# Linear attention and two MLPs: the root by Ln and Exp, other distances in the second batch, hosted x over another tile, earlier stores of the first weights

## The chip, the cores and the metric

The kernel runs on one core of a Trainium2 chip. What is measured is the device time of one execution in microseconds (us). A core has TensorE (PE: matmuls, with their weight loads as PEld), VectorE (DVE), ScalarE (ACT), GpSimd (POOL), and SyncE (SP), whose queue issues most of the DMAs; ACT's queue issues the others. TensorE writes to PSUM, which has eight banks here, and DVE and ACT read its results from there. Each engine works through its instructions in the order in which they stand in its queue: an instruction that waits holds up those behind it.

## The reference

Eight batches of eight heads, 576 rows, 64 columns per head; then two MLPs over 4608 tokens, 512 wide with 2048 inside.

```
kv  = einsum('bhsd,bhse->bhde', k, v)
out = einsum('bhsd,bhde->bhse', q, kv)
x   = out / sqrt(mean(out * out, axis=-1) + 1e-06) * g_norm    # heads side by side: 4608 x 512
h   = x @ w_in1;  g = h if h >= 1, 0 if h <= -1, else (h + 1)**2 / 4;  x = g @ w_out1
h   = x @ w_in2;  g = max(h, 0)**2;                            out = g @ w_out2
```

The weights come in as 64-bit floats, read as pairs of 32-bit words.

## The kernel before, in words

**Products.** A tile that must be multiplied with good precision is split into a high part of type fp32r and a low part, the difference. `mm3` adds three matmuls (high by high, high by low, low by high). Some small products of the attention are done instead as one matmul in full fp32, which the profile shows as two instructions.

**The stages.** The first five batches (`PLAIN`) go through the first MLP plainly, one block each: in each of 16 steps `h_stage` makes one 128-wide slice of h (12 matmuls), `g_stage` splits g, and `out_stage` adds its product into four accumulators (12 matmuls). The first six steps of the first block run ahead of its out stages. After these five blocks come six pairs of batches (`PAIRS`) and a rest, in which both MLPs are done with seven products for a two by two block product (`in_phase`, `out_phase`). These take weights and sums of weights from a DRAM copy in split form (`wsd`), by `load_w2` into tiles `ws`.

**Slots.** A slot is half a step: slot 2t follows the h stage of step t, slot 2t+1 its out stage, and a block has 32 slots. `hook` puts work into a slot. This gives the program's order; a planner then arranges the instructions of each engine by its own estimate of when each is ready, so the order in a queue can differ from that of the program.

**Attention.** A batch has four pairs of heads. Batch 0 goes ahead of the first block (`attention_first` with `t_first`, `o_first`, `r_first`). Batches 1 to 4 go along in the block before their own, and batches 5 to 7 are hosted in the first two pairs: twelve pairs of heads, whose x goes to DRAM (`xpd`, `xrd`). For one pair of heads, starting at slot s: `kv_stage` (k by v into one bank, copied to SBUF), `t_stage` (q transposed by DVE), two `o_stage` halves (q by kv; ACT writes the squares and the product with g, which stands in `gvec` times -0.5), and `r_stage`. For all batches but 0 the PSUM banks are the two buffers of the tag `at`.

**r_stage.** For each half, a matmul with a tile of 1/64 gives the mean square m in a bank (`pr`); ACT makes y = 1/sqrt(|m + 1e-6|) from it, over the squares' tile. Then t = y squared (ACT), o = o * y (DVE), and one Newton step: `newton` makes t = (m + 1e-6) * t (it reads the banks, and frees them), `norm` makes (t - 3) * o, which with gvec's -0.5 is x. It goes over t, and for hosted batches over o, from which it is stored.

**Distances.** In `attention`, pair j starts at s = base + int(every * j), with every 6.7 for batches 1 to 4 and 6 for hosted ones. The o halves are at s+4 and s+5, r at s+8 (s+7 for hosted). Batch 1 calls `kv_stage` for each pair at its s; the others for two pairs at once. Loads stand seven slots ahead of their use (q of hosted pairs: five). `WHOLE` names pairs (1,0) and (1,1), whose squares too are multiplied in full fp32.

**First weights.** `split_w` (slots 2i and 2i+1 of the first block, a few steps ahead of use) makes the split tiles of the first MLP's weights: 16 of w_in, 16 of w_out. Their copies in DRAM are stored by SyncE's queue (line 159). The last nine of w_out (`TAIL`) are stored right after they are split and read again as `wt` tiles by `load_tail` in each later block (line 294). The other 23 are stored by `keep_first`, number j at slot 14 + 2j. Stores of all columns are 512 KB, those of half 256 KB. From the second block on, the second MLP's weights are prepared beside the blocks (`prep_load`, `prep_narrow`, `prep_sums`, `prep_split`; loads at lines 316 and 321) and stored by ACT's queue.

Of the kernel before, what the change touches and what calls it, by code (L numbers as in the profile page):

```python
# [10 lines left out]
F32 = mybir.dt.float32  # L11
F32R = mybir.dt.float32r
AF = mybir.ActivationFunctionType
ALU = mybir.AluOpType
I32 = mybir.dt.int32
BF16 = mybir.dt.bfloat16

# [53 lines left out]
def linear_attention_rms_two_mlps(  # L71
# [112 lines left out]
    ident = ap2.tile([P, P], F32, tag="q", name="ident")  # L184
    ones = const.tile([P, P], F32R, name="ones")
    gvec = const.tile([P, 1], F32, name="gvec")
    epsb = const.tile([P, 1], F32, name="epsb")
    halfb = const.tile([P, 1], F32, name="halfb")
    kv0 = wp.tile([P, NP, P], F32, tag=f"w1_{NF - 1}", name="kv0")
    rests = [const.tile([P, 2, 2, D], F32, name=f"rest{i}") for i in range(2)]  # L190
    kvbd = [const.tile([P, P], F32, name=f"kvbd{i}") for i in range(2)]

    engines = {"A": nc.scalar, "D": nc.vector, "P": nc.gpsimd}
    turns = {op: [itertools.cycle(e) for e in by.split()] for op, by in ENGINES.items()}
# [5 lines left out]
    def engine(op, phase):  # L200
        return engines[next(turns[op][min(phase, 2)])]
# [9 lines left out]
    def copy(e, dst, src):  # L211
        if e is nc.scalar:
            return e.copy(dst, src)  # L213
        if e is nc.vector:
            return e.tensor_copy(dst, src)
        return scaled(e, dst, src, 1.0)
# [249 lines left out]
    def kv_stage(*pairs):  # L466
        ps = bank(pairs[0][0], "pkv_{}_{}".format(*pairs[0]))
        for n, (b, hp) in enumerate(pairs):
            kt, vt = kvm.pop((b, hp))
            r = kvr.pop((b, hp))  # L470


            for c in range(MR + 1):
                for j in range(2):
                    s = slice(j * D, (j + 1) * D)
                    d = slice(n * P + j * D, n * P + (j + 1) * D)
                    lhs, rhs = (kt[:, c, j], vt[:, j, c, :]) if c < MR else (r[0][:, j], r[1][:, j])
                    nc.tensor.matmul(ps[s, d], lhs, rhs, start=c == 0, stop=c == MR)  # L478
        for n, (b, hp) in enumerate(pairs):
            for j in range(2):  # L480
                s = slice(j * D, (j + 1) * D)
                d = slice(n * P + j * D, n * P + (j + 1) * D)
                if b == 0:
                    copy(engine("kv_hi", b), kv0[s, hp, s], ps[s, d])
                    continue
                if (b, hp) in WHOLE:
                    copy(engine("kv_hi", b), kvw[s, hp % 2, s], ps[s, d])
                    continue
                copy(engine("kv_hi", b), kvbd[turn[b, hp] % len(kvbd)][s, s], ps[s, d])

    def t_first(hp):
        qT = scratch(hp, "qT")
# [22 lines left out]
    def newton(t, m):  # L515
        nc.vector.scalar_tensor_tensor(t, m, 1e-6, t, op0=ALU.add, op1=ALU.mult)

    def norm(dst, t, o):
        nc.vector.scalar_tensor_tensor(dst, t, -3.0, o, op0=ALU.add, op1=ALU.mult)

    marks = []

    def r_first(hp):
        y, o = og.pop((0, hp))
        t = scratch(hp, "t")
        ms = []
        for half in range(2):
            ps = bank(0, f"pr_0_{hp}_{half}")
            m = ps[:, :U]
            nc.tensor.matmul(m, ones.bitcast(F32), y[:, half], start=True, stop=True)  # L530
            nc.scalar.activation(y[:, half], m, AF.Abs_reciprocal_sqrt, bias=epsb)
            ms.append(m)
        square(engine("y", 0), t, y)
        nc.vector.tensor_tensor(o, o, y, ALU.mult)
        for half in range(2):
            newton(t[:, half], ms[half])
        norm(t, t, o)
        n = TB // 2
        rem = xrem[0][:, hp, :].rearrange("p (h r) -> p h r", h=2)
        nc.gpsimd.tensor_copy(rem, t[:, :, n:])  # L540
        x = xs[1, 0][hp].rearrange("p a (h n) -> p a h n", h=2)
        marks.append(split(x, t[:, :, :n], "x", 0))


    def t_stage(b, hp):
        work = [ap1.tile([P, S], F32, tag=f"wk{n}", name=f"wk{n}_{b}_{hp}") for n in range(2)]
        qT = ap1.tile([P, S], F32, tag="hl0", name=f"qT_{b}_{hp}")
        nc.vector.transpose(qT, qs.pop((b, hp)))
        hl[b, hp] = (work, qT)

    def o_stage(b, hp, half):
        work, qT = hl[b, hp]
        whole = (b, hp) in WHOLE
        kv = kvw[:, hp % 2, :] if whole else kvbd[turn[b, hp] % len(kvbd)]
        c = slice(half * U, (half + 1) * U)
        ps = bank(b, f"po_{b}_{hp}_{half}")
        nc.tensor.matmul(ps[:, :U], kv, qT[:, c], start=True, stop=True)  # L557
        if whole:
            nc.scalar.activation(work[0][:, c], ps[:, :U], AF.Square)
            scaled(engine("o", b), work[1][:, c], ps[:, :U], gvec)  # L560
            return
        if half == 0:

            og[b, hp] = [ap1.tile([P, S], F32R, tag="wk2", name=f"s2_{b}_{hp}")]
        s2 = og[b, hp]
        nc.scalar.activation(s2[0][:, c], ps[:, :U], AF.Square)
        nc.scalar.activation(work[0][:, c], ps[:, :U], AF.Square)
        scaled(engine("o", b), work[1][:, c], ps[:, :U], gvec)
        if half == 1:
            s2.append(ap1.tile([P, S], F32R, tag="hl1", name=f"s2lo_{b}_{hp}"))  # L570
            lo = engine("sq_lo", b)
            lo.tensor_tensor(s2[1], work[0], s2[0].bitcast(F32), ALU.subtract)

    def r_stage(b, hp):
        (y, o), _ = hl.pop((b, hp))
        if (b, hp) in WHOLE:
            products = [(ones.bitcast(F32), y)]
        else:
            products = [(ones, s2) for s2 in og.pop((b, hp))]
        ms = []  # L580
        for half in range(2):
            c = slice(half * U, (half + 1) * U)
            ps = bank(b, f"pr_{b}_{hp}_{half}")
            m = ps[:, :U]
            for n, (one, s2) in enumerate(products):
                nc.tensor.matmul(m, one, s2[:, c], start=n == 0, stop=n == len(products) - 1)  # L586
            nc.scalar.activation(y[:, c], m, AF.Abs_reciprocal_sqrt, bias=epsb)
            ms.append((c, m))
        pool, tag = (ap1, "wk2") if b < PLAIN else (ap2, "q")
        t = pool.tile([P, S], F32, tag=tag, name=f"t_{b}_{hp}")  # L590
        square(engine("y", b), t, y)
        nc.vector.tensor_tensor(o, o, y, ALU.mult)
        for c, m in ms:
            newton(t[:, c], m)
        if b < PLAIN:
            norm(t, t, o)
            nc.gpsimd.tensor_copy(xrem[b][:, hp, :], t[:, TB:])
            split(xs[1, b][hp], t[:, :TB], "x", b)
            return
        norm(o, t, o)  # L600
        nc.sync.dma_start(xpd[b][:, hp, :], o[:, :TB])
        nc.sync.dma_start(xrd[:, hp, b, :], o[:, TB:])

    def new_x(L, b):
        xs[L, b] = [
# [23 lines left out]
    def attention(base, every, order):  # L629

        slots = []
        for j, (b, hp) in enumerate(order):
            s = base + int(every * j)
            turn.setdefault((b, hp), len(turn))
            if b == 1:
                slots += [(max(0, s - 7), load_kv, b, hp), (s, kv_stage, (b, hp))]
            elif j % 2 == 0:
                two = order[j : j + 2]
                turn.setdefault(two[-1], len(turn))
                slots += [(max(0, s - 7), load_kv, *i) for i in two]  # L640
                slots.append((s - (1 if j else 0) - (b < PLAIN and j > 0), kv_stage, *two))
            slots += [
                (max(0, s - (7 if b < PLAIN or j < 2 else 5)), load_q, b, hp),
                (s, t_stage, b, hp),
                (s + 4, o_stage, b, hp, 0),
                (s + 5, o_stage, b, hp, 1),
            ]
            late = 8 if b < PLAIN else 7
            if j == 0 and b < PLAIN:
                slots.append((s + late, begin, b))  # L650
            slots.append((s + late, r_stage, b, hp))
        if b < PLAIN:
            slots.append((2 * NF * b + 2, store_xrem, b))
        return slots

    def store_xrem(b):
# [426 lines left out]

    jobs = [(8, store_xrem, 0)]
    for b in range(1, PLAIN):
        jobs += attention(2 * NF * (b - 1), 6.7, [(b, hp) for hp in range(NP)])
    for job in sorted(jobs, key=lambda j: j[0]):
        hook(*job)
    for i in range(NF):
# [10 lines left out]
    last = 2 * (PLAIN - 1) * NF  # L1100
    kept = [(w, f) for f in range(NF) for w in range(2) if w == 0 or f < NF - TAIL]
    for j, (w, f) in enumerate(kept):
        hook(14 + 2 * j, keep_first, w, f)

    units = (
# [41 lines left out]
            else:  # L1147
                hook(last + 25, *job)

    nc.scalar.preload_act_table_set("abs_reciprocal_sqrt_and_small")  # L1150
    load_first()
    for f, w in ((2, 0), (3, 0), (0, 1), (4, 0), (1, 1), (5, 0), (2, 1), (6, 0), (3, 1)):
        load_w(1, f, w)
# [12 lines left out]
    for j in range(2):  # L1166
        s = slice(j * D, (j + 1) * D)
        nc.vector.memset(ones[s, s].bitcast(F32), 1.0 / D)
    for t in kvbd:
        nc.vector.memset(t, 0.0)  # L1170
    for t in rests:
        nc.gpsimd.memset(t, 0.0)
    nc.gpsimd.memset(kv0, 0.0)
    nc.vector.tensor_scalar_mul(gvec, gvec, -0.5)
    nc.vector.memset(epsb, 1e-6)
    nc.vector.memset(halfb, 0.5)

    kvw = ap1.tile([P, 2, P], F32, tag="hl1", name="kvw")
# [128 lines left out]
```

## Time and profile before

| | before |
|---|---|
| median of 3 runs | 1578.41 us (1578.3 to 1580.91) |
| the profiled execution's own time | 1577.31 us |
| its span | 1575.5 us |
| PE busy | 1544.7 us, 98% |
| DVE busy | 1169.7 us, 74% |
| ACT busy | 896.1 us, 57% |
| HBM over the span | 245 GB/s |

Busy time is the time in which at least one instruction of the engine runs; matmuls are pipelined, so TensorE can be busy and still not at its peak. Times in the trace are counted from the start of the span. In the rows, "L516" is line 516 of the kernel, "po<-qT,kvbd" reads "tile po written from tiles qT and kvbd", and a bracket with an arrow says how long the engine was idle before the instruction and what ended that.

### The profile page before, as it was taken

The page shows a single profiled execution, that of the slowest core. Times are in us where ns is not written, and L with a number is a line of the kernel's source. Part 1 is how long each engine was busy: PE and PEld are TensorE (multiplying, and loading weights), DVE is VectorE, ACT ScalarE, POOL GpSimd, SP SyncE. Part 2 cuts the span into 40 slices and gives each one's busy share as a digit, 9 for nine tenths or more (in the row PEclk, how much of TensorE's full clock was granted, in tenths as well). Part 3 has the DMA queues.
Part 4 walks back from the last instruction along what each step waited for, and adds up shares of the span by engine and source line. Part 5 has one row for each costly group of instructions (what it writes and reads, how often), then busy time and mean ns, then how long its engine had stood idle before and what let it go on. Part 6 is the DMA issues. An engine that isn't in the chain of part 4 may idle for free.

```text
span 1575.5 us, 22117 instructions
## 1 busy us (share of the span) xinstructions
PE 1544.7 (98%) x7581; PEld 1268.8 (81%) x7581; DVE 1169.7 (74%) x2033; ACT 896.1 (57%) x1693; POOL 10.8 (1%) x30
## 2 busy tenths in 40 slices
PE   9999989999999999998999999999999999999999
PEld 5777768887877788787778888888888888888899
DVE  6975777776789668964789788868884597559666
ACT  5875756666656556734566466546653464446354
POOL 0000000000000000000000000000000000000000
PEclk9999999999999999999999999999999999999999
DMA  9776899897799967789867877776776676977797
GB/s 282 199 231 208 239 338 293 278 288 235 237 341 343 334 200 212 243 226 220 250 187 234 229 240 244 223 218 196 245 233 207 198 242 198 243 243 214 223 391 249
DMA packets 330911, 388.14 MB, mean 246 GB/s; under 512 B 197808, under 2 KB 223408, under 8 KB 330800
## 3 DMA queue, kind: packets, MB, share of 16 engines
q1 hardware_dynamic: 299904, 330.63, 70.1%
q10 hardware_dynamic: 30896, 56.11, 9.8%
q8 instruction: 60, 0.98, 0.2%
q14 instruction: 51, 0.42, 0.1%
HBM read 300.42 MB, written 86.25 MB: 245 GB/s over the span
## 4 chain that ended last, share of the span: by engine, by line
PE 87%; DMA 4%; DVE 4%; ACT 3%; issue 1%; SPq 1%; ACTq 0%; DVEq 0%
PE ph L858 31%; PE po L858 31%; PE acc L234 11%; PE ph L234 10%; PE po L557 2%; DMA wt<-wsd 1%; PE pkv L478 1%; PE pr L586 1%; DMA wsd<-s 1%; DVE s L182 1%; DMA ws<-wsd 1%; DMA v<-in_v_dram 0%; DVE u L684 0%; DMA k<-in_k_dram 0%; DVE x L787 0%
## 5 line engine op out<-in xcount | busy, mean ns | idle before, releaser
L858 PE MATMUL ph<-x,ws 128*128 128x512 f32 (+1 forms) x2352 | 508.7, 377 | 0.5 <-DVE u L684 0.5
L858 PEld LDWEIGHTS ph<-x,ws 128*128 128x128 f32 x2352 | 421.0, 190 | 81.0 <-DVE u L684 0.9
L858 PE MATMUL po<-t,ws 128*128 128x512 f32 x2016 | 462.4, 390 | 0.8 <-DVE t L787 0.8
L858 PEld LDWEIGHTS po<-t,ws 128*128 128x128 f32 x2016 | 377.9, 188 | 80.7 <-DVE t L787 2.2
L787 DVE TENSOR_TENSOR t<-g,t 128x512 fp32r<-128x512 f32 (+1 forms) x336 | 216.3, 649 | 86.4 <-ACT t L213 82.9
L213 ACT CAST t<-g 128x512 fp32r<-128x512 f32 (+1 forms) x336 | 195.5, 590 | 117.7 <-PE po L858 63.3
L234 PE MATMUL ph<-x,w 128*128 128x512 f32 x960 | 241.2, 397 | 8.5 <-DVE u L684 7.4
L234 PEld LDWEIGHTS ph<-x,w 128*128 128x128 f32 x960 | 178.4, 188 | 52.3 <-DVE u L684 10.7
L935 ACT ACTIVATE g<-h 128x512 f32<-128x512 f32 (+1 forms) x120 | 70.6, 589 | 111.8 <-DVE h L924 111.8
L234 PE MATMUL acc<-gs,w 128*128 128x512 f32 x528 | 132.4, 395 | 0.4 <-ACT w L213 0.2
L924 DVE CUSTOM_DVE_ANT_0 h<-ph,e 128x512 f32<-128x512 f32 (+1 forms) x120 | 76.3, 637 | 61.0 <-PE ph L858 56.9
L914 DVE TENSOR_TENSOR e<-ph,e 128x512 f32<-128x512 f32 (+1 forms) x112 | 72.3, 650 | 61.3 <-PE ph L858 56.5
L234 PEld LDWEIGHTS acc<-gs,w 128*128 128x128 f32 x528 | 98.2, 188 | 22.2 <-ACT w L213 0.9
L234 PE MATMUL acc<-gs,wt 128*128 128x512 f32 x432 | 107.6, 398 | 3.9 <-DVE gs L226 2.2
L234 PEld LDWEIGHTS acc<-gs,wt 128*128 128x128 f32 x432 | 82.0, 191 | 22.3 <-DVE gs L226 2.6
L213 ACT CAST gs<-u 128x512 fp32r<-128x512 f32 x80 | 49.7, 622 | 65.0 <-DVE u L684 48.8
L682 ACT ACTIVATE u<-ph,halfb 128x512 f32<-128x512 f32 x80 | 55.2, 690 | 48.0 <-PE ph L234 36.1
L213 ACT CAST x<-xr 128x512 fp32r<-128x512 f32 (+1 forms) x98 | 57.2, 589 | 43.1 <-DVE xr L838 24.3
L226 DVE TENSOR_TENSOR gs<-u,gs 128x512 fp32r<-128x512 f32 x80 | 54.9, 687 | 27.0 <-ACT gs L213 26.5
L684 DVE SCALAR_TENSOR_TENSOR u<-u,ph 128x512 f32<-128x512 f32 x80 | 54.3, 681 | 24.1 <-ACT u L220 24.0
L787 DVE TENSOR_TENSOR x<-xr,x 128x512 fp32r<-128x512 f32 (+1 forms) x98 | 63.1, 648 | 2.6 <-ACT x L213 2.6
L911 ACT COPY e<-ph 128x512 f32<-128x512 f32 (+1 forms) x56 | 30.8, 554 | 56.4 <-PE ph L858 49.5
(127 smaller groups left out, 1547.0 us busy)
## 6 DMA issues: line engine op xcount, KB each, us to landing
ws<-wsd SPq DMA_DIRECT2D x392, 512.0 KB, 4.4
wsd<-s ACTq DMA_DIRECT2D x96, 512.0 KB, 5.5
wt<-wsd SPq DMA_DIRECT2D x36, 512.0 KB, 5.5
raw<-in_moe_w_in_dram SPq DMA_DIRECT2D x32, 512.0 KB, 6.6
raw<-in_moe_w_out_dram SPq DMA_DIRECT2D x32, 512.0 KB, 6.5
xr<-x1d SPq DMA_DIRECT2D x36, 256.0 KB, 5.4
out_dram<-ov SPq DMA_DIRECT2D x142, 64.0 KB, 3.5
wsd<-w SPq DMA_DIRECT2D x17, 512.0 KB, 4.2
```

The lines of the kernel that those rows point to most:

```text
L213: return e.copy(dst, src)
L226: lo = engine(op + "_lo", phase).tensor_tensor(t[:, 1, :], src, t[:, 0, :].bitcast(F32), ALU.subtract)
L234: nc.tensor.matmul(dst, wt(a), xt(c), start=first and n == 0, stop=last and n == 2)
L557: nc.tensor.matmul(ps[:, :U], kv, qT[:, c], start=True, stop=True)
L682: nc.scalar.activation(u, ps, AF.Relu, bias=halfb, scale=0.5)
L684: nc.vector.scalar_tensor_tensor(u, u, 1.0, ps, op0=ALU.min, op1=ALU.max)
L787: engine2(op + "_lo").tensor_tensor(t[:, 1, :], src, t[:, 0, :].bitcast(F32), ALU.subtract)
L858: nc.tensor.matmul(ps, wt(a), xt(c), start=first and n == 0 and i == 0, stop=last and n == len(lhs) - 1 and i == 2, skip_group_check=True,)
L911: nc.scalar.copy(e[i, 1], bank)
L914: nc.vector.tensor_tensor(e[i, p], bank, e[i, 1], ALU.add)
L924: nc.vector._custom_dve(TENSOR_ADD_SAT, out=h, in0=bank, in1=add, s0=float("inf"), s1=0.0)
L935: nc.scalar.activation(g, h, AF.Square)
```

## The change

The root: y is made as exp(-0.5 * ln(m + 1e-6)), Ln for each half from the bank, Exp once over both halves. Ln's input is scaled by 2^-44, and Exp's bias takes that back. The product of o and y is gone; `norm` makes t = (t - 3) * y and then t = o * t, and hosted x is stored from t. ACT's table is preloaded for the new functions.

The second batch (batch 1): for pairs (1,2) and (1,3) kv and the transposed q are split, and o is made by `mm3`. For all its pairs every is 7, the o halves are at s+3 and s+4, r at s+6. The other batches keep their distances.

The stores: `keep_first` number j stands at slot 16 + int(2j / 3).

```diff
-    epsb = const.tile([P, 1], F32, name="epsb")
+    lnb = const.tile([P, 1], F32, name="lnb")
+    expb = const.tile([P, 1], F32, name="expb")
...
+    kv1 = const.tile([P, 2, P], F32R, name="kv1")
...
-                copy(engine("kv_hi", b), kvbd[turn[b, hp] % len(kvbd)][s, s], ps[s, d])
+                if b > 1:
+                    copy(engine("kv_hi", b), kvbd[turn[b, hp] % len(kvbd)][s, s], ps[s, d])
+                    continue
+                t = kv1
+                copy(engine("kv_hi", b), t[s, 0, s], ps[s, d])
+                nc.vector.tensor_tensor(t[s, 1, s], ps[s, d], t[s, 0, s].bitcast(F32), ALU.subtract)
...
-    def norm(dst, t, o):
-        nc.vector.scalar_tensor_tensor(dst, t, -3.0, o, op0=ALU.add, op1=ALU.mult)
+    def norm(t, y, o):
+        nc.vector.scalar_tensor_tensor(t, t, -3.0, y, op0=ALU.add, op1=ALU.mult)
+        nc.vector.tensor_tensor(t, o, t, ALU.mult)
... r_first
-            nc.scalar.activation(y[:, half], m, AF.Abs_reciprocal_sqrt, bias=epsb)
+            nc.scalar.activation(y[:, half], m, AF.Ln, bias=lnb, scale=LN_SCALE)
             ms.append(m)
+        nc.scalar.activation(y, y, AF.Exp, bias=expb, scale=-0.5)
         square(engine("y", 0), t, y)
-        nc.vector.tensor_tensor(o, o, y, ALU.mult)
         for half in range(2):
             newton(t[:, half], ms[half])
-        norm(t, t, o)
+        norm(t, y, o)
... t_stage
-        qT = ap1.tile([P, S], F32, tag="hl0", name=f"qT_{b}_{hp}")
+        if b > 1 or (b, hp) in WHOLE:
+            qT = ap1.tile([P, S], F32, tag="hl0", name=f"qT_{b}_{hp}")
+            nc.vector.transpose(qT, qs.pop((b, hp)))
+            hl[b, hp] = (work, qT)
+            return
+        qT = ap1.tile([P, S], F32, tag="wk2", name=f"qf_{b}_{hp}")
+        parts = [ap1.tile([P, S], F32R, tag=f"hl{n}", name=f"qT{n}_{b}_{hp}") for n in range(2)]
         nc.vector.transpose(qT, qs.pop((b, hp)))
-        hl[b, hp] = (work, qT)
+        copy(engine("q_hi", b), parts[0], qT)
+        engine("q_lo", b).tensor_tensor(parts[1], qT, parts[0].bitcast(F32), ALU.subtract)
+        hl[b, hp] = (work, parts)
... o_stage
+        if b > 1:
+            nc.tensor.matmul(
+                ps[:, :U], kvbd[turn[b, hp] % len(kvbd)], parts[:, c], start=True, stop=True
+            )
+        else:
+            mm3(ps[:, :U], lambda a: kv1[:, a, :], lambda a: parts[a][:, c], True, True)
... r_stage
-            nc.scalar.activation(y[:, c], m, AF.Abs_reciprocal_sqrt, bias=epsb)
+            nc.scalar.activation(y[:, c], m, AF.Ln, bias=lnb, scale=LN_SCALE)
             ms.append((c, m))
+        nc.scalar.activation(y, y, AF.Exp, bias=expb, scale=-0.5)
...
-        nc.vector.tensor_tensor(o, o, y, ALU.mult)
         for c, m in ms:
             newton(t[:, c], m)
         if b < PLAIN:
-            norm(t, t, o)
+            norm(t, y, o)
...
-        norm(o, t, o)
-        nc.sync.dma_start(xpd[b][:, hp, :], o[:, :TB])
-        nc.sync.dma_start(xrd[:, hp, b, :], o[:, TB:])
+        nc.vector.scalar_tensor_tensor(t, t, -3.0, y, op0=ALU.add, op1=ALU.mult)
+        nc.vector.tensor_tensor(t, o, t, ALU.mult)
+        nc.sync.dma_start(xpd[b][:, hp, :], t[:, :TB])
+        nc.sync.dma_start(xrd[:, hp, b, :], t[:, TB:])
... attention
-                (s + 4, o_stage, b, hp, 0),
-                (s + 5, o_stage, b, hp, 1),
+                (s + 3 + (b > 1), o_stage, b, hp, 0),
+                (s + 4 + (b > 1), o_stage, b, hp, 1),
             ]
-            late = 8 if b < PLAIN else 7
+            late = 6 + (b > 1) + (1 < b < PLAIN)
...
-            slots.append((2 * NF * b + 2, store_xrem, b))
+            slots.append((2 * NF * b + 2 * (b > 1), store_xrem, b))
...
-        jobs += attention(2 * NF * (b - 1), 6.7, [(b, hp) for hp in range(NP)])
+        jobs += attention(2 * NF * (b - 1), 6.7 if b > 1 else 7, [(b, hp) for hp in range(NP)])
...
-    hook(14 + 2 * j, keep_first, w, f)
+    hook(16 + 2 * j // 3, keep_first, w, f)
...
-    nc.scalar.preload_act_table_set("abs_reciprocal_sqrt_and_small")
+    nc.scalar.preload_act_table_set("natural_log_exp_and_others")
```

## Rows read from the trace of the kernel before

**Rows 1.** The page's busy shares: us, share of the span, instructions

```profile
PE 1544.7 (98%) x7581; PEld 1268.8 (81%) x7581; DVE 1169.7 (74%) x2033; ACT 896.1 (57%) x1693; POOL 10.8 (1%) x30
```

**Rows 2.** Windows, first block: length; PE, PEld, DVE, ACT, POOL busy; clock, DMA share, GB/s

```profile
36.00:56.00 20.00, 19.32 (x98) 14.54 (x96) 19.62 (x37) 18.13 (x34) 0.64 (x1) 1.00 0.90 239
...
sum 100.00, PE 98.34 PEld 76.51 DVE 84.55 ACT 79.47 POOL 2.12; mean PE 19.67 PEld 15.30 DVE 16.91 ACT 15.89 POOL 0.42
```

**Rows 3.** Windows, first block's end and second block; columns as above

```profile
120.00:130.00 10.00, 9.70 (x40) 6.88 (x39) 8.62 (x17) 6.65 (x12) 0.37 (x1) 1.00 0.39 144
...
190.00:200.00 10.00, 6.52 (x29) 4.80 (x28) 8.24 (x16) 7.53 (x17) 0.00 (x0) 0.99 0.71 204
200.00:210.00 10.00, 6.39 (x18) 4.79 (x18) 5.38 (x10) 4.77 (x9) 0.24 (x1) 0.67 1.02 348
210.00:220.00 10.00, 9.73 (x42) 7.99 (x43) 8.98 (x18) 3.19 (x7) 0.00 (x0) 1.00 0.95 328
```

**Rows 4.** Timeline in the second block: start us, us, instruction, idle before it

```profile
200.85 0.63 ACT L220 ACTIVATE u<-u 128x512 f32<-128x512 f32 x1 [1.82 <-DVE s L355]
...
202.26 0.80 PE L234 MATMUL ph<-x,w 128*128 128x512 f32 x1 [5.73 <-DVE u L684]
```

**Rows 5.** Chain that ended last, second block: start us, us, what

```profile
142.94 0.73 PE pkv L478 x20
...
164.01 2.72 PE acc L234 x12
...
171.72 1.02 PE po L557 x4
...
229.33 0.53 PE pr L586 x4
```

**Rows 6.** Timeline of SyncE's queue, blocks one and two

```profile
118.05 13.41 SPq L159 DMA_DIRECT2D wsd<-w  x6
...
131.50 0.84 SPq L418 DMA_DIRECT2D k<-in_k_dram  x1
...
182.49 8.11 SPq L159 DMA_DIRECT2D wsd<-w  x3
...
201.30 0.94 SPq L294 DMA_DIRECT2D wt<-wsd  x1
```

**Rows 7.** Waits of SyncE's queue, 60 to 245 us: total, times, longest

```profile
SPq L159 <- DVE d L266: 35.9, 4, 14.1
...
SPq L159 <- DMA wsd<-s: 18.8, 5, 6.0
```

**Rows 8.** Timeline of TensorE beside the pairs

```profile
724.75 1.66 PE L557 MATMUL po<-qT,kvbd 128*128 128x288 f32 x4 [2.50 <-DVE t L516]
...
791.43 1.33 PE L557 MATMUL po<-qT,kvbd 128*128 128x288 f32 x2 [3.04 <-DVE qT L548]
```

**Rows 9.** Waits of SyncE's queue, 530 to 840 us

```profile
SPq L601 <- DVE wk L519: 22.4, 8, 4.5
```

**Rows 10.** Groups by line: busy us, mean ns, idle before

```profile
L587 ACT ACTIVATE wk<-pr,epsb 128x288 f32<-128x288 f32 x56 | 26.4, 502 | 7.1 <-PE pr L586 6.5
...
L220 ACT ACTIVATE t<-wk 128x576 f32<-128x576 f32 x28 | 19.3, 689 | 0.5
...
L519 DVE SCALAR_TENSOR_TENSOR t<-t,wk 128x576 f32<-128x576 f32 x16 | 12.1, 754 | 0.1
...
L1150 ACT ACT_TABLE_LOAD x1 | 1.3, 1283 | 0.7 <-PEq L1285 0.7
```

**Rows 11.** Timeline of ACT, start of the first block

```profile
37.40 0.62 ACT L213 CAST x<-t 128x512 fp32r<-128x512 f32 x1 [1.78 <-DVE t L519]
```

**Rows 12.** Timeline, r_stage of pair (1,2)

```profile
105.81 0.40 PE L586 MATMUL pr<-s,ones 128*128 128x288 f32 x1
...
108.30 0.82 DVE L516 SCALAR_TENSOR_TENSOR t<-pr,t 128x288 f32<-128x288 f32 x2
```

More of the change, by code (lines that the diff above doesn't have):

```diff
@@ L16 @@
 BF16 = mybir.dt.bfloat16
+LN_SCALE = 2.0**-44
+LN2 = 0.6931471805599453
 REBIAS = 2.0**-112
@@ L546, in t_stage @@
         work = [ap1.tile([P, S], F32, tag=f"wk{n}", name=f"wk{n}_{b}_{hp}") for n in range(2)]
-        qT = ap1.tile([P, S], F32, tag="hl0", name=f"qT_{b}_{hp}")
+        if b > 1 or (b, hp) in WHOLE:
[5 more added lines that the diff above has]
+        parts = [ap1.tile([P, S], F32R, tag=f"hl{n}", name=f"qT{n}_{b}_{hp}") for n in range(2)]
         nc.vector.transpose(qT, qs.pop((b, hp)))
-        hl[b, hp] = (work, qT)
+        copy(engine("q_hi", b), parts[0], qT)
+        engine("q_lo", b).tensor_tensor(parts[1], qT, parts[0].bitcast(F32), ALU.subtract)
+        hl[b, hp] = (work, parts)
     def o_stage(b, hp, half):
-        work, qT = hl[b, hp]
-        whole = (b, hp) in WHOLE
-        kv = kvw[:, hp % 2, :] if whole else kvbd[turn[b, hp] % len(kvbd)]
+        work, parts = hl[b, hp]
         c = slice(half * U, (half + 1) * U)
-        ps = bank(b, f"po_{b}_{hp}_{half}")
-        nc.tensor.matmul(ps[:, :U], kv, qT[:, c], start=True, stop=True)
-        if whole:
+        if (b, hp) in WHOLE:
+            ps = bank(b, f"po_{b}_{hp}_{half}")
+            nc.tensor.matmul(
+                ps[:, :U], kvw[:, hp % 2, :], parts[:, c], start=True, stop=True
+            )
             nc.scalar.activation(work[0][:, c], ps[:, :U], AF.Square)
@@ L565, in o_stage @@
         s2 = og[b, hp]
+        ps = bank(b, f"po_{b}_{hp}_{half}")
+        if b > 1:
+            nc.tensor.matmul(
+                ps[:, :U], kvbd[turn[b, hp] % len(kvbd)], parts[:, c], start=True, stop=True
+            )
+        else:
+            mm3(ps[:, :U], lambda a: kv1[:, a, :], lambda a: parts[a][:, c], True, True)
         nc.scalar.activation(s2[0][:, c], ps[:, :U], AF.Square)
@@ L1168, in linear_attention_rms_two_mlps @@
         nc.vector.memset(ones[s, s].bitcast(F32), 1.0 / D)
-    for t in kvbd:
+    for t in kvbd + [kv1.bitcast(F32)]:
         nc.vector.memset(t, 0.0)
@@ L1174, in linear_attention_rms_two_mlps @@
     nc.vector.tensor_scalar_mul(gvec, gvec, -0.5)
-    nc.vector.memset(epsb, 1e-6)
+    nc.vector.memset(lnb, LN_SCALE * 1e-6)
+    nc.vector.memset(expb, -22.0 * LN2)
     nc.vector.memset(halfb, 0.5)
```

## The prediction

> **What bounds the kernel now.** I read the page's busy shares first, then the span in windows, then the PE timeline where a window fell short, then the queue that feeds it. The reader sees TensorE busy 98% of the span, ACT 57%, DVE 74% [rows 1]. So an added ACT or DVE instruction costs only where TensorE waits for that engine or for a PSUM bank that it must empty, and a saved wait pays fully only on TensorE. There are three such places.
>
> The first block: in 36 to 56 us DVE is busy 19.6 and ACT 18.1 of 20 us, while from 36 to 136 they are at 84.6 and 79.5 of 100 and TensorE still runs 98.3 [rows 2]. Nothing is lost yet, but little room is left.
>
> The second block: TensorE works 6.52, 6.39 and 9.73 us in three windows of 10 from 190 to 220, at 0.67 of the granted clock in the middle one, between its two levels [rows 3]. The longest wait there is 5.73 us for DVE's u [rows 4]. The idle time is 30 - 22.64 = 7.4 us. In the middle window 18 matmuls took 6.39 us, 0.355 each; twelve in 2.72 us [rows 5] is 0.227 each; so 18 x 0.128 = 2.3 us went to the slow clock. The place is worth at most 9.7 us. SyncE is late there: three stores of first weights hold its queue for 8.1 us from 182.5, and a tail-weight load goes out at 201.3 only [rows 6]. In 60 to 245 us stores of L159 waited 18.8 us for other DMAs and 35.9 us for DVE [rows 7].
>
> The hosted attention beside the pairs: TensorE waits 2.50 us for the step that empties PSUM (newton, L516) and 3.04 us for a transpose that DVE runs between newton's halves [rows 8]; SyncE waits 22.4 us in 8 places for L519 before storing hosted x [rows 9].
>
> **The change part by part.** The sum is made against the profiled execution, 1577.31 us, whose span is 1575.5; 1.8 us lie around it. The median shown is 1578.41, 1.1 us more, which I add at the end.
>
> *The root.* Each of 32 pairs (4 first, 16 in batches 1 to 4, 12 hosted) gets one Exp over 576 columns more on ACT; Ln takes the place of the old function at equal shape, at 0.50 us [rows 10], assumed equal. The trace has no Exp: below it is bounded by the 576-wide Square, 0.69, above by two half-width passes with a bias, 1.00; I take 0.75, nearer the former, 24 us on ACT in all. DVE keeps its count: the product with o, which ran beside the Square, goes, and t times o comes behind norm, at 0.75 [rows 10]. So the path from the sum of squares to x grows by 0.75 + 0.75 = 1.5 us, and to newton, which frees the banks, by 0.75.
>
> In the first block four pairs pay this ahead of the first x. ACT waited 1.78 us for the last t [rows 11], so it can take two Exps in its stride, and TensorE starts on the other x tiles first. Zero below; above, 1.5 for the chain and 1.5 for two Exps ahead of it, 3.0. I take **+1.0**.
>
> For batches 2 to 4 the distances don't change. Newton comes 0.75 later, and the next o stage is two half-steps or more behind: 24 matmuls, 5.4 us, against 3.3 + 0.75 from pr to newton's end [rows 12]. I take 0, with up to +4 if a third of the 12 pairs waits for the whole Exp.
>
> *Second batch.* Pairs (1,2) and (1,3) take three products of type fp32r instead of one in full fp32. Four fp32 instructions (two halves) took 1.02 us; fp32r ones at 288 columns 0.53 for four, 0.13 each [rows 5]. Six of them are 0.80: 0.2 us less per pair, **-0.4** in all. For it ACT gets two q copies (0.7 each), DVE two q subtractions (0.75) and four small ones of kv. With the four Exps this is 4.4 us more for ACT and about 2.4 for DVE, in the block where both are near full. All serial would be 6.8, all hidden 0. I take **+2.5**: a third falls where the engines are full, and u and gs queue behind it, for which TensorE waits.
>
> The distances: r goes from s+8 to s+6, the next kv_stage comes at s+7 instead of s+6 (6.7 rounded). So far r's two banks of the pair `at` were asked for next by an o stage two slots behind; now kv_stage asks one slot behind, after 12 matmuls, 2.72 us. The first bank is free when newton's first half is done: 3.3 - 0.4 + 0.75 = 3.65 us. 0.9 us is short, at three places, 2.8 us; none if the planner puts other matmuls ahead. I take **+2.0**.
>
> *Stores.* Of 23 stores through `keep_first`, the first nine keep to the first block; fourteen (numbers 9 to 22, slots 32 to 58) move from the second block into slots 22 to 30. With the nine of the tail, all 32 (of which the code makes 17 whole and 15 half tiles) are then issued there. The first block has the room for the bytes: the DMA share is 0.39 in 120 to 130 [rows 3]. But on SyncE they are queued with k, v and q of batch 2 at slot 25. These already leave at 131.5, behind six stores that took 13.4 us [rows 6], waiting for DVE. Eight more stores than before come ahead of them (numbers 6 to 13). At 0.5 us each and mostly inside waits that exist, I take **+1.5** for batch 2's start; 0 below; above, eight whole stretches like the six (2.2 us each) less the waits that were there, about 6.
>
> What goes is fourteen stores from the second block. Of the 9.7 us lost there, I take back **-4**: SyncE is freer by 182, but ACT's part of u waited 1.82 us at 200.85 for second-layer preparation ordered in front of it on DVE [rows 4], and this order I expect to stay. Bounds: 0 and -9.7. What would be late next is that preparation.
>
> *Hosted x* is written over t in the pool `q` and stored from there; o's tile comes free after the last product instead of after the stores. The next q takes the other of that pool's two buffers, so I cost the tile at 0; the load behind it would otherwise wait for a store. But xpd and xrd are issued 1.5 us later for each of 12 pairs, on SyncE, which already stands 22.4 us there and has the `ws` loads behind. These run ahead of their use, so most is hidden: 1.0 us. TensorE's waits of 2.50 and 3.04 each grow by 0.75: 1.5. Together **+2.5**; 0 below, +8 if half of the 18 us of longer standing comes through.
>
> Sum: 1.0 - 0.4 + 2.5 + 2.0 + 1.5 - 4.0 + 2.5 = +5.1; 1582.4, and on the median's footing **1583.5**.
>
> A rule that speaks against the root: the Trainium skill, page "ScalarE: Activation LUTs", section "Table sets: the hidden batching unit", says that functions are loaded as sets, that Ln and Exp share one, and that cheap functions are in every set; among these it names relu, copy, identity and abs, and neither Square nor Prelu. In the trace one load of a table, 1.28 us, stands in the whole trace, with Square and Prelu in use [rows 10]. By the rule as it stands for named functions the sum is unchanged; by its silence on the two it is the last rival.
>
> **Rivals.**
> 1. *The second block's stall goes altogether* (faster). For it: SyncE's lateness there and the store waits. Against it: DVE and ACT order. -9.7 instead of -4, and the first-block terms at half (3.3 instead of 6.6): 1583.5 - 5.7 - 3.3 = 1574.5.
> 2. *Costs and gain cancel* (no change): the terms of the first block are hidden by the planner's order, the rest holds: 1583.5 - 5 = 1578.5.
> 3. *The first block's SyncE queue is overfull*: k, v and q of batch 2 come 6 us late, TensorE stands and its clock falls as at 200 us (2.3 us), and the second block gives nothing back: 1583.5 + 4.5 + 2.3 + 4 = 1594. It decides from the point where the eight loads of batch 2's first two pairs leave more than 2 us later than from 131.5 on: their pkv runs at 142.9 [rows 5], an estimate.
> 4. *The change doesn't do what it says: tables are switched*, twice a pair, 64 x 1.28 = 82 us on ACT, about a third of it on the path: 1610.
>
> **How the numbers follow.** Forecast 0.40 (its own range 1581 to 1589), rival 1 0.24, rival 2 0.21, rival 3 0.13, rival 4 0.02. A difference of under 0.2%, 3.2 us, can't be told from none. Faster is rival 1, 0.24; same is rival 2, 0.21; slower is the forecast and rivals 3 and 4, 0.55. The range reaches into rivals 1 and 3: 1572 to 1596.
>
> **What would show it.** Root: one Exp of 0.7 to 0.8 us per pair and one table load; the first x some 1 to 1.5 us later. Banks: TensorE's pkv of batch 1 idle before it, released by L516. Stores: 32 by 135 us, none after; the second block's wait of 5.7 us shorter than 4. Hosted: waits for newton at 3.2 us or more. Wrong would be: TensorE idle in the first 130 us as before, or no wait over 1 us between 140 and 250.

## The result and the profile after

The changed kernel takes 1593.47 us (median of 4 runs, 1590.87 to 1595.26) against 1579.66 us for the kernel before on the same chip (4 runs, 1578.3 to 1582.27): a ratio of 1.0084 [1.0063, 1.0105], 13.8 us slower. The forecast of 1583.5 had the side right and the size not: it said some 5 us, two of its terms were wrong by about 10 us each and a third by 7. The profiled execution has a span of 1591.0 us.

The page's busy shares of the changed kernel, as [rows 1] of the kernel before:

```profile
PE 1548.5 (97%) x7585; PEld 1269.5 (80%) x7585; DVE 1170.9 (74%) x2041; ACT 916.3 (58%) x1727; POOL 11.0 (1%) x30
```

TensorE's work is nearly the same (3.8 us more busy time, part of it at a slower clock); ACT is busy 20 us more, by the Exps. The span grew by 15.5, so most of it is TensorE standing still or slow. Where, the windows show: first block, its end, and the second block (as [rows 2, 3]).

```profile
36.00:56.00 20.00, 18.07 (x94) 13.60 (x92) 19.53 (x37) 17.60 (x34) 0.24 (x1) 1.00 0.88 258
...
sum 100.00, PE 97.92 PEld 77.52 DVE 85.62 ACT 81.93 POOL 2.11; mean PE 19.58 PEld 15.50 DVE 17.12 ACT 16.39 POOL 0.42
```

```profile
120.00:130.00 10.00, 10.00 (x46) 8.03 (x46) 8.47 (x16) 8.40 (x16) 0.00 (x0) 1.00 0.47 184
190.00:200.00 10.00, 7.22 (x31) 5.33 (x28) 5.04 (x9) 6.74 (x15) 0.37 (x1) 0.66 0.93 262
200.00:210.00 10.00, 4.18 (x15) 2.84 (x15) 9.45 (x18) 7.42 (x16) 0.00 (x0) 0.88 0.68 248
210.00:220.00 10.00, 10.00 (x37) 8.03 (x37) 3.77 (x9) 4.42 (x9) 0.00 (x0) 0.78 0.80 254
```

The first block is full as before: 97.9 of 100 us against 98.3. The second block is worse: from 190 to 220 us TensorE works 21.4 of 30 us (22.6 before), and the granted clock, 0.67 in one of these windows before and full in the others, is at 0.66, 0.88 and 0.78. To place the loss I count the main 128x512 matmuls of the blocks by their order. The first one starts 1.4 us earlier than before (27.98 against 29.37 us), the 577th still 5.6 us earlier (180.80 against 186.42), the 673rd 5.7 us later (226.45 against 220.75), the 769th 7.6 later. Then nothing happens until the hosted pairs: the 2689th is 4.1 us late (737.03), the 2785th 12.2 (771.14), the last of them some 15. So the time was lost in two places, 185 to 250 us and 735 to 860 us.

The second block, by TensorE's waits (timeline: start, duration, instruction, idle before it; before, [rows 4]):

```profile
189.52 0.69 PE L487 MATMUL pkv<-v,k 128*64 128x64 f32 x16 [2.25 <-DMA v<-in_v_dram]
...
193.95 4.62 PE L243 MATMUL ph<-x,w 128*128 128x512 f32 x12 [1.83 <-DVE u L715]
...
206.74 0.40 PE L616 MATMUL pr<-s2lo,ones 128*128 128x288 f32 x1 [2.15 <-DVE s2lo L602]
...
209.14 2.08 PE L243 MATMUL ph<-x,w 128*128 128x512 f32 x4 [2.00 <-DVE u L715]
```

No wait is as long as the 5.73 us of before, but there are more of them, and the first is for a load of v. Twelve matmuls take 4.62 us here; at 175.36 us, at the full clock (1.00 from 170 to 180 us), twelve such take 2.88. Why v was late, SyncE's queue shows (as [rows 6]):

```profile
108.16 23.49 SPq L166 DMA_DIRECT2D wsd<-w  x12
131.69 1.14 SPq L427 DMA_DIRECT2D k<-in_k_dram  x1
...
137.77 2.88 SPq L443 DMA_DIRECT2D q<-in_q_dram  x4
154.32 7.47 SPq L166 DMA_DIRECT2D wsd<-w  x10
161.89 1.24 SPq L325 DMA_DIRECT2D raw<-in_moe_w_in_dram  x2
...
180.49 0.39 SPq L430 DMA_DIRECT2D v<-in_v_dram  x1
...
195.08 2.41 SPq L303 DMA_DIRECT2D wt<-wsd  x1
```

and its waits from 60 to 245 us (total, times, longest; as [rows 7]), with ACT's own queue beside them:

```profile
SPq L166 <- DVE w L189: 31.5, 4, 16.0
SPq L166 <- DMA x1d<-ev: 14.4, 2, 13.6
SPq L430 <- DMA wsd<-s: 10.2, 1, 10.2
```

```profile
151.25 0.57 ACT L752 COPY ev<-acc 128x512 f32<-128x512 f32 x1
151.84 0.35 ACTq L181 DMA_DIRECT2D x1d<-ev  x1
```

Batch 2's first k leaves at 131.69 as before (131.50). But nine of the moved stores stand behind the last tail store, and that one waits 13.6 us for a transfer which ACT can issue only at 151.84, when the first block's accumulators have been copied out. What it waits for last is a counter. In the trace SyncE's 1000 transfers and ACT's 123 name the same eight counters, and each waits until the transfer before it on its counter has landed. For this store that is ACT's of 151.84, which lands at 154.26. Everything queued on SyncE behind it stands too: raw, q, k, v, and the wt tiles. The v that leaves at 180.49 then stands 10.2 us more in the same way, for a store of second-layer weights (`wsd<-s`) that ACT issues at 177.73 and that lands at 180.43; the v that TensorE waits for at 189.52 leaves behind it, at 184.90.

The hosted pairs. DVE beside them, changed kernel, then the kernel before:

```profile
752.61 0.82 DVE L530 SCALAR_TENSOR_TENSOR t<-pr,t 128x288 f32<-128x288 f32 x2
753.97 0.75 DVE L630 SCALAR_TENSOR_TENSOR t<-t,wk 128x576 f32<-128x576 f32 x1
755.33 0.75 DVE L631 TENSOR_TENSOR t<-wk,t 128x576 f32<-128x576 f32 x1
755.99 0.77 DVE L564 STREAM_TRANSPOSE qT<-q 128x576 f32<-128x576 f32 x1
```

```profile
749.20 0.77 DVE L548 STREAM_TRANSPOSE qT<-q 128x576 f32<-128x576 f32 x1
750.48 0.76 DVE L592 TENSOR_TENSOR wk<-wk,wk 128x576 f32<-128x576 f32 x1 [0.51 <-ACT wk L587]
751.20 0.82 DVE L516 SCALAR_TENSOR_TENSOR t<-pr,t 128x288 f32<-128x288 f32 x2
752.05 0.76 DVE L519 SCALAR_TENSOR_TENSOR wk<-t,wk 128x576 f32<-128x576 f32 x1
```

Before, the next pair's q transpose runs ahead of the root's chain; now it runs behind the chain's last instruction. TensorE, which ran from 750 to 780 us without a gap, has the first three of these waits there; the fourth is two pairs later, where it stood 3.04 us before [rows 8], and there too the transpose runs behind the chain:

```profile
756.82 1.00 PE L591 MATMUL po<-qT,kvbd 128*128 128x288 f32 x2 [2.13 <-DVE qT L564]
...
764.12 0.40 PE L616 MATMUL pr<-s,ones 128*128 128x288 f32 x1 [1.58 <-ACT wk L214]
765.30 0.53 PE L616 MATMUL pr<-s2lo,ones 128*128 128x288 f32 x2 [0.79 <-DVE s2lo L602]
...
804.46 1.33 PE L591 MATMUL po<-qT,kvbd 128*128 128x288 f32 x2 [5.24 <-DVE qT L564]
```

SyncE's wait ahead of xpd hardly moved: 24.5 us in 7 places (22.4 in 8, [rows 9]):

```profile
SPq L632 <- DVE t L631: 24.5, 7, 5.5
```

The root's instructions cost what was assumed (groups by line, as [rows 10]: busy, mean ns, idle before):

```profile
L617 ACT ACTIVATE wk<-pr,lnb 128x288 f32<-128x288 f32 x56 | 26.4, 502 | 11.6 <-PE pr L616 11.5
L619 ACT ACTIVATE wk<-wk,expb 128x576 f32<-128x576 f32 x28 | 21.9, 783 | 2.8 <-DMA q<-in_q_dram 2.5
...
L1181 ACT ACT_TABLE_LOAD x1 | 1.3, 1283 | 0.7 <-PEq L1317 0.7
```

### The profile page after: what moved, and what is told of

Its sections match the earlier page's. It is cut to its first block, busy times and chain, and to the rows that moved or that the text cites. A ratio compares the mean times of both kernels' runs of the same rounds, so it can differ in the third digit from the quotient of the medians.

```text
span 1591.0 us, 22177 instructions
## 1 busy us (share of the span) xinstructions
PE 1548.5 (97%) x7585; PEld 1269.5 (80%) x7585; DVE 1170.9 (74%) x2041; ACT 916.3 (58%) x1727; POOL 11.0 (1%) x30
## 4 chain that ended last, share of the span: by engine, by line
PE 84%; DVE 7%; DMA 4%; ACT 3%; issue 1%; SPq 0%; ACTq 0%; DVEq 0%
PE ph L889 31%; PE po L889 29%; PE acc L243 10%; PE ph L243 9%; PE po L591 1%; PE pkv L487 1%; DMA v<-in_v_dram 1%; DVE s L189 1%; DMA wt<-wsd 1%; PE pr L616 1%; DMA k<-in_k_dram 1%; DVE u L715 1%; DVE t L818 1%; DMA ws<-wsd 1%; DVE x L818 1%
## 5 line engine op out<-in xcount | busy, mean ns | idle before, releaser
L243 PEld LDWEIGHTS ph<-x,w 128*128 128x128 f32 x960 | 179.7, 190 | 51.5 <-DVE u L715 10.1
L222 ACT CAST x<-xr 128x512 fp32r<-128x512 f32 (+1 forms) x98 | 57.2, 589 | 45.7 <-DVE xr L869 24.5
```

The source lines that it names most:

```text
L243: nc.tensor.matmul(dst, wt(a), xt(c), start=first and n == 0, stop=last and n == 2)
```

## The experiments

Medians stand beside those of the kernel before on the same chip: 1578.95 us for the first four, 1579.95 for the next four, 1580.54 for the last four. Ratios are to it.

**e1: the stores spread as before.**

```diff
-    hook(16 + 2 * j // 3, keep_first, w, f)
+    hook(14 + 2 * j, keep_first, w, f)
```

> The changed kernel with keep_first back at slot 14 + 2j. Theory S (the early stores: SyncE's queue holds ten of them from 140.6 to 161.8 us, so that v, q and the tail weights of the second block come late): most of the 13 us lost between 180 and 207 us go, ratio to before 1.000 to 1.003, and TensorE is no later than before at the end of the second block. Theory R (the longer root: r_stage's chain and the added ACT work): the stall stays, 1.006 to 1.009. In both the 7.5 us lost in the hosted stretch from 733 to 860 stay if they come from the root.

Measured: 1588.5 us, 1.0051 [1.0028, 1.0074]. The second block loses nothing (769th matmul 1.6 us early); from 733 to 766 us it goes from 0.8 early to 7.3 late. So the early stores cost, and most of the rest is lost beside the hosted pairs.

**e2: the kernel before with the early stores alone** (the edit of e1 the other way round).

> The kernel before with keep_first at slot 16 + 2j // 3 alone. Theory S: the second block loses about 8 to 13 us more than before, ratio 1.004 to 1.008, the hosted stretch as before. Theory R: the stores free the second block, 0.996 to 1.000.

Measured: 1584.84 us, 1.0036 [1.0021, 1.0052]. At the 577th matmul it is 3.3 us early, at the 769th 7.5 late; nothing is lost later. TensorE's waits in the second block now name the loads:

```profile
190.84 1.12 PE L478 MATMUL pkv<-v,k 128*64 128x64 f32 x16 [1.46 <-DMA v<-in_v_dram]
...
217.59 4.58 PE L234 MATMUL acc<-gs,wt 128*128 128x512 f32 x12 [3.49 <-DMA wt<-wsd]
```

The term that I had at -2.5 (+1.5 and -4.0) is a loss, with no other edit near.

**e3: the kernel before with the root alone**, in all batches; hosted x still over o's tile.

```diff
-            nc.scalar.activation(y[:, c], m, AF.Abs_reciprocal_sqrt, bias=epsb)
+            nc.scalar.activation(y[:, c], m, AF.Ln, bias=lnb, scale=LN_SCALE)
...
+        nc.scalar.activation(y, y, AF.Exp, bias=expb, scale=-0.5)
-        nc.vector.tensor_tensor(o, o, y, ALU.mult)
...
-        norm(o, t, o)
+        nc.vector.scalar_tensor_tensor(t, t, -3.0, y, op0=ALU.add, op1=ALU.mult)
+        nc.vector.tensor_tensor(o, o, t, ALU.mult)
```

> The kernel before with Ln and Exp and the product with o behind norm, hosted x still over o's tile. Theory R: 1.004 to 1.009, with the loss at both places. Theory S: the second block as before within 3 us; only the hosted stretch is longer, by 2 to 8 us, 1.001 to 1.005.

Measured: 1575.39 us, 0.9977 [0.9964, 0.9991]: a gain of 3.6 us. The first main matmul starts at 27.70 us, 1.7 earlier. Beside the hosted pairs 3.2 us are gained: the 2641st matmul is 2.6 us late, the 3169th 0.6 early. In place of the waits of 2.50 and 3.04 us in [rows 8] TensorE has one:

```profile
791.24 1.33 PE L562 MATMUL po<-qT,kvbd 128*128 128x288 f32 x2 [2.60 <-DVE t L520]
```

Some 2.3 us are lost between the 1201st and the 1345th matmul, in the fourth block. e8, below, shows the same three: 1.5 us at the start, 3.2 beside the hosted pairs, 2.5 lost between. The profiled execution of e3 took 2.5 us more than the kernel's median (its span is 1576.1 us), so these parts don't add up to the 3.6.

**e4: the kernel before with the second batch's split and distances alone** (its edits in the diff above, nothing else).

> The kernel before with batch 1's split products and distances alone. Both theories: no loss; the first block ends 1 to 4 us earlier as it does in the changed kernel, ratio 0.997 to 1.000. A third theory, that these distances move the planner's order in the second block so that the stall grows: 1.004 or more.

Measured: 1580.8 us, 1.0013 [0.9999, 1.0028]: 1.9 us slower, which can't be told from none; the trace has it 0.9 us late at 247 us.

**e5: the kernel before with hosted x over t alone.**

```diff
-        norm(o, t, o)
-        nc.sync.dma_start(xpd[b][:, hp, :], o[:, :TB])
-        nc.sync.dma_start(xrd[:, hp, b, :], o[:, TB:])
+        norm(t, t, o)
+        nc.sync.dma_start(xpd[b][:, hp, :], t[:, :TB])
+        nc.sync.dma_start(xrd[:, hp, b, :], t[:, TB:])
```

> The kernel before with one edit: hosted x written over t (in the pool q) and stored from there. Theory (tile): the loss of 7 to 9 us beside the pairs, which the kernel with the old store slots still had and the root alone had not, belongs to this tile: 1586 to 1589 against 1579, TensorE 7 us or more later between 735 and 775 us than in the kernel before, the next pair's q transpose behind norm on DVE. Rival (tile and root together): norm's end comes late enough to matter only with the longer root, so alone the tile gives 1578 to 1580. My costing in the prediction: 0, thus 1579.

Measured: 1589.04 us, 1.0058 [1.0038, 1.0078]. The instruction counts are those of the kernel before, and DVE and ACT are busy as long (1169.5 and 897.2 us); only the tile differs. It goes from 2.5 us late at the 2641st matmul (715 us) to 11.4 late at the 2785th, with the q transpose behind the chain as in the changed kernel:

```profile
752.56 0.82 DVE L516 SCALAR_TENSOR_TENSOR t<-pr,t 128x288 f32<-128x288 f32 x2
...
753.92 0.75 DVE L519 SCALAR_TENSOR_TENSOR t<-t,wk 128x576 f32<-128x576 f32 x1
...
755.28 0.77 DVE L548 STREAM_TRANSPOSE qT<-q 128x576 f32<-128x576 f32 x1
```

**e6: e3 with hosted x over t.** The edit is e5's.

> The kernel before with the root by Ln and Exp for all batches and hosted x over t; old distances, old store slots. Theory (tile) and rival (tile and root together) alike: 1575.4 of the root alone plus 7 to 9, so 1582 to 1585. If it stays at 1575 to 1577, neither holds: the loss beside the pairs would then come with the second batch's split or distances, through the order in which the later work is laid out.

Measured: 1588.04 us, 1.0055 [1.0037, 1.0072]; by the ratios 12.3 us more than the root alone, more than either theory said. The rival, that the tile costs only together with the root, had fallen with e5.

**e7: the changed kernel with hosted x over o.**

```diff
-        nc.vector.tensor_tensor(t, o, t, ALU.mult)
+        nc.vector.tensor_tensor(o, o, t, ALU.mult)
```

(and the two stores read o)

> The changed kernel with hosted x written over o again and stored from o; all else as changed. If the tile costs 7 to 9: 1593.5 less 8, so 1585 to 1587, with the loss of 12 us in the second block unchanged. If the loss beside the pairs is not the tile's: 1592 to 1595.

Measured: 1583.49 us, 1.0020 [1.0009, 1.0030]; the hosted stretch gains 2.1 us (7.4 late at the 2641st matmul, 5.3 at the 3169th), and the second block loses nearly as much as in the changed kernel (from 5.7 early to 6.5 late; 5.6 to 7.6 there).

**e8: e7 with the stores at their old slots** (e1's edit).

> The changed kernel with hosted x over o and the stores at their old slots (14 + 2j): the root, the split and the distances of the second batch stay. If losses add: 1593.5 less 8 (tile) less 5 to 7 (stores), 1578 to 1581, near the kernel before; by the terms of the two single edits, -3.5 for the root and +1.9 for the second batch, 1577. If the second batch's split and distances carry the loss beside the pairs, 1585 to 1589.

Measured: 1575.9 us, 0.9976 [0.9964, 0.9988]. This is root, split and distances; it equals the root alone, so beside the root the second batch's part costs nothing that can be measured.

**e9 and e10: which of the two tiles.** With x over t, o's tile comes free at the end of norm, and t is held until the stores have landed. e9 frees o and t (it holds s2lo's tile instead); e10 holds both.

```diff
# e9
-        norm(o, t, o)
+        norm(products[1][1], t, o)
+        x = products[1][1].bitcast(F32)
... stores read x
# e10
-        norm(o, t, o)
+        norm(o[:, :TB], t[:, :TB], o[:, :TB])
+        norm(t[:, TB:], t[:, TB:], o[:, TB:])
... xpd reads o, xrd reads t
```

> The kernel before with hosted x written over the tile of the squares' low part (s2lo, so x is rounded to fp32r), and stored from there: neither o's tile nor the pool q is held until the stores land. Theory (o comes free): once o's tile is free after norm, the planner puts the chain of the pair that has it (o*y, newton, norm) ahead of the next pair's q transpose on DVE, and TensorE waits for the transpose; the loss stays, 1586 to 1590, 8 us or more later at 785 us than the kernel before. Rival (t held): the pool q's tile, held until the stores, is what changes the order; here it isn't held: 1578 to 1581.

> The kernel before with the first 512 columns of hosted x written over o and the last 64 over t, each stored from there (one small DVE instruction more per hosted pair, some 0.2 us): both tiles are held until the stores land. Theory (o comes free): o is held as before, so the order is as before, 1579 to 1582. Rival (t held): 1586 to 1590.

Measured: e9 1591.13 us, 1.0071 [1.0054, 1.0088]; e10 1579.72 us, 0.9992 [0.9979, 1.0005]. DVE's order at the same pair, e9 and then e10:

```profile
753.35 0.82 DVE L516 SCALAR_TENSOR_TENSOR t<-pr,t 128x288 f32<-128x288 f32 x2 [0.33 <-ACT t L220]
754.27 0.76 DVE L519 SCALAR_TENSOR_TENSOR s2lo<-t,wk 128x576 fp32r<-128x576 f32 x1
754.95 0.77 DVE L548 STREAM_TRANSPOSE qT<-q 128x576 f32<-128x576 f32 x1
```

```profile
750.59 0.77 DVE L548 STREAM_TRANSPOSE qT<-q 128x576 f32<-128x576 f32 x1
751.86 0.76 DVE L592 TENSOR_TENSOR wk<-wk,wk 128x576 f32<-128x576 f32 x1 [0.51 <-ACT wk L587]
```

It is o's release that brings the loss, not the hold on t. Where o is held (before, e10) the transpose runs first, where it is free (e5, e9) the chain does, whichever other tile is held. What o's hold bounds, the trace of the kernel before shows: the next pair's product with g writes that tile, and waits for the store.

```profile
758.29 0.89 ACT L205 ACTIVATE wk<-po,gvec 128x288 f32<-128x288 f32 x2 [1.26 <-DMA xrd<-wk]
```

That o's release turns the order is shown; why the planner then puts the chain ahead of the transpose is not seen in a trace.

**e11 and e12: the 23 stores of keep_first issued from POOL's queue**, on e7 (early slots) and on e8 (old slots).

```diff
-        keep_halves(1, which, f % NH, f // NH, t.bitcast(F32), now=True)
+        keep_halves(1, which, f % NH, f // NH, t.bitcast(F32), now=True, by=nc.gpsimd)
```

> The changed kernel with hosted x over o (1583.5) and the 23 early stores through keep_first issued from POOL's queue in place of SyncE's; same slots. Theory (SyncE's queue): the loss of 12 us in the second block is that of the loads queued on SyncE behind the moved stores, which stand there from 140 to 162 us and wait for other queues' transfers; without them the second block loses nothing, 1574 to 1577, TensorE's waits there under 3 us. Rival (bytes): the stores' traffic in the first block and the early second delays the loads wherever it is issued: 1582 to 1585. My prediction costed the moved stores at -2.5 in sum, so 1577 at the changed kernel's other terms.

> As e11, with the stores at their old slots (14 + 2j), so against 1575.9 for the same kernel with SyncE issuing them. If SyncE's queue still costs in the second block there: 1568 to 1573, with TensorE's idle time between 190 and 220 us (7.4 in the kernel before) halved. If DVE's order sets that stall, as I held for part of it: 1574 to 1577.

Measured: e11 1563.53 us, 0.9898 [0.9878, 0.9918]; e12 1561.83 us, 0.9891 [0.9870, 0.9913]. Both are faster than the kernel before and the changed kernel, and the gain is larger than either theory said. e11's windows, to be read against [rows 3], and its SyncE queue:

```profile
190.00:200.00 10.00, 10.00 (x47) 8.32 (x47) 7.10 (x13) 7.33 (x15) 0.00 (x0) 1.00 0.90 274
200.00:210.00 10.00, 10.00 (x45) 8.18 (x44) 9.45 (x18) 8.73 (x19) 0.63 (x1) 1.00 1.07 335
210.00:220.00 10.00, 10.00 (x47) 8.30 (x47) 6.88 (x15) 5.24 (x10) 0.00 (x0) 1.00 0.87 279
```

```profile
127.51 0.62 SPq L427 DMA_DIRECT2D k<-in_k_dram  x1
...
135.91 0.38 SPq L166 DMA_DIRECT2D wsd<-w  x1
136.40 1.28 SPq L325 DMA_DIRECT2D raw<-in_moe_w_in_dram  x2
...
169.73 0.97 SPq L303 DMA_DIRECT2D wt<-wsd  x1
```

TensorE works 30.0 of 30 us at the full clock; the raw loads leave 25.5 us earlier than in the changed kernel, the first wt 25.4. The same bytes move, with a DMA share as high (1.07 in one window), so the bytes were not the limit. The stores' slot no longer matters: both kernels lead the kernel before by 12.8 to 12.9 us after the second block, where the same kernels with SyncE's stores were 6.5 (e7) and 0.3 us (e8) late. By the ratios the whole gain is 19.3 us over e7 and 13.4 over e8, so nearly all of it is made by then.

What of the move does it is not told apart. The last tail store, which waited 13.6 us in the changed kernel, is still on SyncE, and now leaves at 135.91 without that wait. POOL's 23 transfers use eight counters of their own, so that SyncE's come to stand on others (the tail store does); they are out of SyncE's queue; and they go over a DMA queue that the changed kernel doesn't use (`q0`, 8.13 MB in 2352 packets by e11's page).

## Why the prediction was right in its side and wrong in its size

Adding the parts one after another, by the ratios times 1579.7 us: root -3.6 (e3), split and distances -0.2 (e8), stores +7.0 (e7), hosted tile +10.1 (the changed kernel); 13.3 of the 13.8 measured. Counted in other kernels the stores come to +5.7 (e2) and +5.2 (e1), the tile to 9.2 to 12.3.

That the side came out right is luck. The terms that were to make the kernel slower, the longer root and the second batch, gave -3.8 together: with them alone (e8) it is faster than before; the two parts that did cost stood in the sum at -2.5 and at 0. One of the prediction's own signs of being wrong came true: TensorE is idle in the first block as before (2.1 us from 36 to 136 us against 1.7), and where the first-block terms added up to +6.6, the 385th matmul, at the end of these 100 us, is 1.8 us early.

*The root*, forecast +1.0 in the first block and, by its longer chain, +2.5 beside the hosted pairs: measured -3.6 in all. The instruction prices were right (Exp 0.78 for 0.75, Ln 0.50, one table load). Wrong was that the chain's length sets the start: in the changed kernel as in e3 the first main matmuls stand on TensorE ahead of a `pr` of the first batch (27.99 and 28.57 us) that they stood behind before (28.45 and 29.37), and start 1.4 to 1.7 us earlier. The root isn't needed for that: e4, which has the old root, starts 1.4 us earlier too, in another order. Beside the hosted pairs the two waits of [rows 8], which were to grow by 0.75 us each, became one of 2.60: 3.2 us gained in e3 and e8, where 2.5 lost was forecast. For batches 2 to 4, put at 0 (up to +4), e3 and e8 lose 2.3 to 2.5 us in the fourth block; the changed kernel, with the same root, loses 0.3 there, so it isn't the chain's length alone. How these parts make 3.6 stays open. The last rival, table switches, is out: the Trainium skill's page "ScalarE: Activation LUTs", section "Table sets: the hidden batching unit", names neither Square nor Prelu as common to all sets; here both run beside Ln and Exp with the one load of 1.28 us.

*Second batch*, forecast -0.4 +2.5 +2.0: measured +1.9 alone, nothing beside the root. ACT and DVE did fill up (81.9 and 85.6 of 100 us, from 79.5 and 84.6), and TensorE lost 0.4 us. The bank wait did not come: the one long wait of TensorE's from 36 to 140 us is 1.5 us for u; pkv of pairs (1,1), (1,2) and (1,3), at 61.97, 79.02 and 106.75, has no idle time of TensorE before it, and the 0.35 us ahead of its weight loads stand there in the kernel before too (78.62, 105.08).

*Stores*, forecast +1.5 for batch 2's start and -4.0 in the second block: measured +7. This step failed twice. I said that all 32 would be issued by 135 us; ten left at 154 to 162: they stand behind batch 2's loads, because the order in SyncE's queue is the planner's and not the slots', and there the first of them waited 13.6 us. And I gave the second block's stall partly to DVE's order, which I expected to stay: without those stores on SyncE it is gone altogether (e11, e12). What I read in [rows 7] as store waits, 18.8 us for other DMAs, was the mechanism itself: a store that waits for another queue's transfer holds every load behind it. Moving the stores earlier in the same queue put nine of them at once, behind a tail store that waited, in front of the loads that the second block starts with.

*Hosted x*, forecast 0 for the tile: measured +10.1 (by ratios 9.2 alone, 12.3 beside the root). I asked who waits for the tile that is now held, and found nobody, rightly (e9, e10). I did not ask what the tile that comes free lets the planner reorder.

Rival 3 gave 1594, but its point was not reached (k of batch 2 left on time). An overfull queue of SyncE's is what the stores brought, only later, in the second block, and for 7 us; that rival 3's figure is near the result is chance: 10 of the 13.8 us are the tile's.

## What to carry to other kernels

Look at what a store waits for in the queue that feeds the critical loads, its completion counter included, since all loads behind it wait with it: moving 23 stores to another engine's queue, with other counters, took 19 us off (ratio 1.0020 to 0.9898), while moving them earlier in the same queue cost 7. Where a planner orders the work, a tile that is released earlier is a change of order too: look at what may now run first, and whether that is what the bound engine waits for. A rise in the price of one instruction can matter less than the order that it brings: with the root alone ACT is busy 20.7 us more, and the kernel is 3.6 us faster.

## What was unexpected of the hardware

Issuing 23 plain stores from POOL's queue instead of SyncE's was worth 19 us. The Trainium skill, page "DMA: Bandwidth & Descriptors", section "Issuing engines are not separate DMA queues", says that starting transfers on several engines "will only save the time on the sequencer it takes to initiate the DMA, which is usually small relative to the DMA itself". The trace agrees that issuing is cheap (ten stores in 7.47 us at 154 us). The runs don't bear out that issue time is all that is saved: what went with the move were waits, such as the 13.6 us that the first of the ten stood with all others behind it, and TensorE's idle time from 190 to 220 us, 8.5 us in e7 and none in e11.

The granted clock was below full where TensorE had gaps and just behind them. From 190 to 220 us it was 0.66, 0.88 and 0.78 in the changed kernel, means between its two levels, with 2.8 and 5.8 us of idle time in the first two windows and none in the third; in e11, without any idle time, it was 1.00 in all three. Twelve matmuls took 4.62 us in the one (at 193.95) and 2.88 in the other:

```profile
190.28 2.88 PE L243 MATMUL ph<-x,w 128*128 128x512 f32 x12
```
